# A second home for half of the attention outputs, and operand builds cut into casts and low parts

## The chip, the cores and the metric

The kernel runs on one core of a Trainium2 chip. The metric is device time in microseconds (us) of one execution. Before the change the median of three timed runs is 581.33 us (580.94 to 581.66).

The engines have short names in the profile: PE is TensorE (matrix products), PEld its weight loads, DVE is VectorE, ACT is ScalarE, POOL is GpSimd, and SP is SyncE, which here only issues transfers. Each engine runs its own instructions in the order in which the program lists them.

## The reference, cut to what matters

Attention with a decay goes over blocks and carries a state; its result x, with the heads side by side, goes through a mixer that works first over tokens and then over channels. All is float32.

```python
# attention: B=4, H=8, S=768, D=64; lam per head, about 0.97 to 0.99
for b in range(nb):                                   # blocks of 64 rows
    intra = (qb @ kb.T * Dmask) @ vb                  # Dmask[i, j] = lam ** (i - j), i >= j
    inter = (qb * lam_pow) @ kv_state
    out[:, :, sl] = intra + inter
    kv_state = lam_block * kv_state + (kb * rev_pow).T @ vb
# mixer: x is (4, 768, 512)
u  = x + (relu(x.T @ w_tok1) @ w_tok2).T              # 768 -> 256 -> 768, over tokens
h2 = relu(u @ w_ch1) @ w_ch2                          # 512 -> 1536 -> 512, over channels
return u + h2
```

## The kernel before, in words

Float32 values that go through the fast form of a matrix product (type fp32r) are split in two parts: a high part `...h`, which ScalarE makes as a cast, and a low part `...l`, the difference of the value and its high part, which VectorE or GpSimd makes. A product is then three products: high by high, high by low, low by high. Results lie transposed in the tiles `uT`, one for each of the 4 batches.

**Pairs.** The first stage goes over 16 pairs (batch, two heads), in the loop over `i` at L620. In step `i` TensorE computes the scores of pair `i + 1` (`sc`, L299), then the first half of the outputs of pair `i` (`xT`, three chunks of 128 rows, L323 and L333), then the state's products of the next pair (`kv`, L265), then the second half of the outputs (`outputs(i, 1)`). ScalarE copies each half from PSUM to `uT` (L340). VectorE scans the state's products (`sv`, L273). After that come transposes of later keys (`kt`, up to pair 7) and queries (`qt`, up to pair 4), transposes back of `uT` (`xp`, L355, read by ScalarE for `xhi` and VectorE for `xlo`), and pieces of the token mixer of earlier batches: `ph` (hidden, L447, read by ScalarE for `hh` and VectorE for `hl`) and `pu` (output, L484, added to `uT` by VectorE at L489). The list `groups` holds these pieces, and `take` says how many a step takes.

**PSUM.** There are eight banks. Three rotate under the tag `sh` (kt, qt, kv, xp, ph, pu, and later the products pa, pb, pc). One has the tag `xT`, used by both halves of the outputs and later by pd. Four are two double banks `sc`. A tile that takes a bank waits until the readers of the bank's last tile are done: under `sh` that is the tile three uses back, under `xT` the one before.

**Units.** The channel mixer is cut into 24 units (a group of 256 of the 1536 hidden channels, one batch): batches 0 and 1 in units 0 to 11, batches 2 and 3 in units 12 to 23. A unit multiplies two by two blocks with seven products (`m1` to `m7`) in place of eight. Their moving operands for a batch are B11, B21, B22, which are blocks of `uT`, and T1 to T4, which come from differences of blocks (`t1` to `t4`). The function `build` (L557) returns these steps, each as a call; `part` (L576) makes a high part on ScalarE and a low part on VectorE (`on_vector`) or GpSimd. For batches 2 and 3 the operands take the tiles of batches 0 and 1, and the differences lie in the tile `cs`, so their rows read `cs<-uT`. The products leave PSUM by s (a copy on ScalarE, L789), u2 and u3 (L794 and L807), c22, c21, c12 (VectorE, L812, L818, L823, all printed as `c`), and then become h11, h21, h12, h22 with their high and low parts. Between the products of unit n stand the four output pairs of unit n - 1 (`po`, L836, added to `uT` by VectorE at L851): m1, m6, pair 0, pair 1, m2, m7, m5, pair 2, m4, pair 3, m3. Pair 0 and pair 1 need h11 and h21, pairs 2 and 3 need h12 and h22. m2, m7 and m3 add to the banks of m1, m6 and m5, and wait until these have been read.

**What sets the order.** The order is written out by hand (a manual schedule). During the pairs a queue `waiting` holds small steps, and `later(n)` takes n from it, and one more when over five wait. In a unit `background(n)` gives a list of (when, step): a product counts 6 and an output pair 12, and a step is issued after the slot at which the count reaches its `when`. For batch 0 the steps are put in `waiting` at i = 13 (L701); for batch 1 they stand in the two lists named `order` (L712 and L734) and in units 0 and 1; for batches 2 and 3 in units 10 to 12 (NP1 is 12).

Of the kernel before, what the change touches and what calls it, by code (L numbers as in the profile page):

```python
# [22 lines left out]
def kernel(  # L23
# [40 lines left out]
    waiting = deque()  # L64

    def later(n):
        n += len(waiting) > 5
        for _ in range(min(n, len(waiting))):
            waiting.popleft()()

# [244 lines left out]
    def outputs(i, g):  # L315
        b, p = pairs[i]
        st = stb[i % 2]
        xT = bank("xT", f"xT{i}{g}", 3 * P)
        for cg in range(3):
            c = 3 * g + cg  # L320
            cs = slice(cg * P, (cg + 1) * P)
            for h in range(2):
                nc.tensor.matmul(  # L323
                    out=xT[h * D : (h + 1) * D, cs],
                    lhsT=vns[i][:, h, c, :],
                    rhs=weights_of[i, g, h][:, cg, :],
                    start=(cg == 0),
                    stop=False,
                )
            if c == 0:  # L330
                continue
            for h in range(2):
                nc.tensor.matmul(  # L333
                    out=xT[h * D : (h + 1) * D, cs],
                    lhsT=st[:, c - 1, h, :],
                    rhs=qss[i][:, c - 1, :],
                    start=False,
                    stop=(cg == 2),
                )
        nc.scalar.copy(out=uT[b][:, p, 3 * g * P : (3 * g + 3) * P], in_=xT)  # L340
# [216 lines left out]
    def build(b, n, temps=None, on_vector=()):  # L557
# [18 lines left out]
        def part(o, src):  # L576
            where = [home(n, o, x) for x in "hl"]
            ops[b][o] = hi, lo = [
                pool.tile([P, 2, SB], F32R, tag=tag, bufs=bufs, name=f"{o}{x}{b}")
                for x, (pool, tag, bufs) in zip("hl", where)  # L580
            ]
            nc.scalar.copy(out=hi, in_=src)
            eng = nc.vector if o in on_vector else nc.gpsimd
            eng.tensor_sub(out=lo, in0=src, in1=hi.bitcast(F32))

        return {
            "t1": lambda: temp("h", b12, b11),
            "t2": lambda: temp("l", b22, t["h"]),
            "t3": lambda: temp("m", b22, b12),
            "t4": lambda: sub(out=t["l"], in0=t["l"], in1=b21),  # L590
            "B11": lambda: part("B11", b11),
            "B21": lambda: part("B21", b21),
            "B22": lambda: part("B22", b22),
            "T1": lambda: part("T1", t["h"]),
            "T2": lambda: part("T2", t["l"]),
            "T3": lambda: part("T3", t["m"]),
            "T4": lambda: part("T4", t["l"]),
        }

    weights = {}  # L600
# [19 lines left out]
    for i in range(-2, NI):  # L620
# [28 lines left out]
        for n in range(3):  # L649
            for f in work[cuts[n] : cuts[n + 1]]:  # L650
                f()
                later(2 if len(work) < 3 else 1)
            if n < 2 and i >= 0:
                turn_back(i, n)
                later(1 if work or i == NI - 1 and n == 0 else 2 + n)
            if n == 0 and i + 2 < NI:
                scale_k(i + 2)
        if i == -1:
# [39 lines left out]
        if i == 11:  # L698
            later(99)
        if i == 13:  # L700
            waiting.extend(first[x] for x in ("t1", "t2", "T2", "T1", "t3", "T3", "t4", "T4", "B22"))  # L701
    later(99)
    att.close()
    ch = ctx.enter_context(tc.tile_pool(name="ch", bufs=1, reuse_waits="tile"))
# [4 lines left out]
        return cp.tile([P, SB], F32, tag="tmp", bufs=5, name=nm)  # L709

    parts = build(1, 1, on_vector=("T2", "T3"))
    order = [[parts["B11"]], [], [parts["t1"]], [parts["t2"], parts["B21"]]]  # L712
    for fs in order:
        groups.popleft()()
        for f in fs:
# [11 lines left out]
    def piece_steps(x):  # L727
# [4 lines left out]
    steps = {}  # L732
    pa = piece_steps(0)
    order = [  # L734
        [parts["T2"], pa[0]],
        [pa[1], pa[2], parts["T1"]],
        [pa[3], pa[4], parts["t3"], lambda: fetch(1, 2)],
        [parts["T3"]],
    ]
    for n, fs in enumerate(order):  # L740
        token_out_pair(B - 1, n // 2, 2 * (n % 2))
# [179 lines left out]
    def background(n):  # L921
# [7 lines left out]
        if n == 0:  # L929
            c1, pb = steps["c1"], piece_steps(1)  # L930
            add(12, pb[0], pb[1], c1[0])
            add(24, pb[2])
            add(36, parts["t4"])
            add(42, pb[3], pb[4], lambda: fetch(1, 3), c1[1])
        if n == 1:
            c1 = steps["c1"]
            add(12, parts["T4"])
            add(24, c1[2], c1[3], c1[4], c1[5])
            add(36, c1[6], parts["B22"])
# [32 lines left out]
                    add(84, lambda: save(to - 1))  # L972
        if n == NP1 - 2:
            second["a"] = bl = build(2, 0, cs_temps(), on_vector=("T1", "T2", "T3", "T4"))
            add(12, bl["t1"], bl["B11"])
            add(24, bl["t2"])
            add(36, bl["T2"])
            add(48, bl["t3"])
            add(60, bl["T3"])
            add(72, bl["T1"])  # L980
            add(84, bl["B21"])
        if n == NP1 - 1:
            al = second["a"]
            second["b"] = bl = build(3, 1, cs_temps(), on_vector=("T1", "T2", "T3", "T4"))
            add(6, al["t4"])
            add(12, al["T4"], al["B22"])
            add(24, bl["t1"], bl["B11"])
            add(36, bl["t2"])
            add(48, bl["T2"])
            add(72, bl["t3"], bl["T3"])  # L990
        if n == NP1:
            bl = second["b"]
            add(12, bl["T1"])
            add(24, bl["t4"])
            add(36, bl["T4"])
            add(36, bl["B21"])
            add(48, bl["B22"])
        if NP1 + 1 <= n < NP1 + 9:
            x = n - NP1 - 1
            add(36, lambda: store(x // 4, x % 4))  # L1000
# [75 lines left out]
```

## Time and profile before

| | |
|---|---|
| median of the runs | 581.33 us |
| the profiled execution's own time | 581.56 us |
| its span (first to last instruction) | 579.8 us |
| TensorE busy | 558.5 us, 96% |
| VectorE busy | 403.5 us, 70% |
| ScalarE busy | 215.9 us, 37% |
| GpSimd busy | 222.4 us, 38% |
| data moved to and from HBM | 67.1 MB, 116 GB/s over the span |

How to read its lines. A row of the waits says who waited for whom, how long in total, how often, and the longest. A row of a timeline has start and length in us, engine, line, operation, result<-inputs, shapes and count; in brackets is the engine's idle time ahead of it and what ended it. A row of the windows has the stretch, its length, and for PE, PEld, DVE, ACT and POOL the busy time with the count, then the share of TensorE's clock that was granted, the share in which the DMA engines were busy, and GB/s. The 16 pairs lie before 188 us of the span together with the token mixer, unit 0 starts at 187.91, unit 10 at 338.26, unit 13 at 389.31.

### The profile page before, as it was taken

To read this page: it belongs to the slowest core of one execution; us is meant where nothing else is said; L and a number is where in the kernel's file an instruction comes from. 1 tells how busy PE (TensorE), PEld (TensorE's weight loads), DVE (VectorE), ACT (ScalarE), POOL (GpSimd) and SP (SyncE) were. 2 spreads that over 40 slices of the span, in tenths; PEclk is the share of its full clock that TensorE was granted. 3 is DMA by queue.
4 is the path that set the end of the run, shared out by engine and by line. 5 is a ranking of instruction groups with operands and counts; after the bars stand their busy time and mean duration, and the time that the engine had idled before them with its cause. 6 is when DMAs were issued, how large, how long until landed. Compare 5 with 4: busy or idle time off the path is not lost. (4 is left out here: it accounts for less than half of the span.)

```text
span 579.8 us, 10666 instructions
## 1 busy us (share of the span) xinstructions
PE 558.5 (96%) x4234; PEld 540.3 (93%) x4234; DVE 403.5 (70%) x602; ACT 215.9 (37%) x426; POOL 222.4 (38%) x200
## 2 busy tenths in 40 slices
PE   5998999999989999999999998999999999999995
PEld 4888898999979999999999998999999999999994
DVE  4787877787777879887778787875455454444554
ACT  3464423435253554444434434451222222222221
POOL 5666632736214554534444453542112122222210
PEclk9998999999999999999999999999999999999999
DMA  9999999797002512352717200002444343540237
GB/s 184 258 227 187 190 198 215 138 161 141 1 2 83 216 71 86 128 217 58 288 38 272 73 0 1 0 1 47 136 115 134 97 147 93 153 101 1 42 48 129
DMA packets 176592, 67.80 MB, mean 117 GB/s; under 512 B 163616, under 2 KB 166816, under 8 KB 176544
## 3 DMA queue, kind: packets, MB, share of 16 engines
q1 hardware_dynamic: 172800, 65.85, 46.3%
q10 hardware_dynamic: 3744, 1.28, 0.9%
q8 instruction: 33, 0.54, 0.4%
q14 instruction: 15, 0.12, 0.1%
HBM read 49.29 MB, written 17.83 MB: 116 GB/s over the span
## 5 line engine op out<-in xcount | busy, mean ns | idle before, releaser
L851 DVE TENSOR_TENSOR uT<-po,uT 128x768 f32<-128x768 f32 x94 | 89.7, 955 | 70.1 <-PE po L836 69.8
L772 ACT ACTIVATE c<-c 128x384 f32<-128x384 f32 x72 | 37.9, 526 | 123.2 <-DVE c L812 54.4
L774 POOL TENSOR_TENSOR h22l<-c,h22h 128x384 fp32r<-128x384 f32 x24 | 25.0, 1040 | 127.8 <-ACT h22h L773 127.8
L286 POOL COPY stb<-sv 64x320 f32<-64x320 f32 x32 | 27.3, 853 | 45.0 <-DVE sv L273 44.1
L774 POOL TENSOR_TENSOR h21l<-c,h21h 128x384 fp32r<-128x384 f32 x24 | 27.4, 1142 | 32.9 <-ACT h21h L773 25.8
L774 POOL TENSOR_TENSOR h12l<-c,h12h 128x384 fp32r<-128x384 f32 x24 | 24.9, 1038 | 38.1 <-PE pa L761 19.2
L323 PE MATMUL xT<-a,vn 128*64 128x128 f32 x384 | 36.8, 284 | 1.8 <-ACT uT L340 1.4
L340 ACT COPY uT<-xT 128x384 f32<-128x384 f32 x32 | 15.3, 478 | 53.9 <-PE xT L333 53.9
L794 DVE TENSOR_TENSOR u<-pb,s 128x384 f32<-128x384 f32 x24 | 13.4, 557 | 28.9 <-PE pb L761 17.2
L307 DVE TENSOR_TENSOR a<-sc,mask 128x768 f32<-128x768 f32 x32 | 29.2, 950 | 6.1 <-PE sc L299 6.0
L800 ACT ACTIVATE h11h<-pa 128x384 fp32r<-128x384 f32 x24 | 11.7, 487 | 58.4 <-PE pa L761 58.4
L333 PE MATMUL xT<-qs,stb 128*64 128x128 f32 x320 | 31.8, 276 | 0.0
L447 PE MATMUL ph<-xhi,w1h 128*128 128x256 f32 x96 | 28.5, 297 | 1.8 <-DVE uT L489 1.5
L323 PEld LDWEIGHTS xT<-a,vn 128*64 128x64 f32 x384 | 22.4, 137 | 6.0 <-ACT uT L340 3.1
L375 POOL TENSOR_TENSOR c1l<-cs,c1h 128x512 fp32r<-128x512 f32 x15 | 19.3, 1296 | 21.8 <-ACT c1h L374 21.8
L299 PE MATMUL sc<-qT,kT 64*128 64x128 f32 x384 | 27.1, 290 | 0.2 <-ACT qT L237 0.2
L447 PE MATMUL ph<-xhi,w1l 128*128 128x256 f32 x96 | 27.1, 283 | 0.0
L447 PE MATMUL ph<-xlo,w1h 128*128 128x256 f32 x96 | 27.1, 282 | 0.0
L299 PEld LDWEIGHTS sc<-qT,kT 64*128 64x128 f32 x384 | 23.9, 196 | 3.3 <-issue 1.8
L252 POOL TENSOR_TENSOR qs<-qT,lamp 128x640 f32<-128x640 f32 x16 | 25.3, 1583 | 0.3
L364 DVE TENSOR_TENSOR xlo<-xp,xhi 128x384 fp32r<-128x384 f32 x32 | 17.6, 551 | 10.3 <-ACT xhi L363 10.3
L836 PE MATMUL po<-h21h,c2h 128*128 128x384 f32 x64 | 21.6, 338 | 0.7 <-ACT h21h L773 0.7
(273 smaller groups left out, 1884.1 us busy)
## 6 DMA issues: line engine op xcount, KB each, us to landing
raw<-in_moe_w_ch_dram SPq DMA_DIRECT2D x20, 512.0 KB, 4.0
vn<-in_v_dram SPq DMA_DIRECT2D x16, 384.0 KB, 5.2
kn<-in_k_dram SPq DMA_DIRECT2D x30, 192.0 KB, 4.7
out_dram<-y SPq DMA_DIRECT2D x110, 48.0 KB, 1.8
qn<-in_q_dram SPq DMA_DIRECT2D x44, 96.0 KB, 3.3
kr<-in_k_dram SPq DMA_DIRECT2D x32, 96.0 KB, 2.9
dc1h<-c1h SPq DMA_DIRECT2D x4, 768.0 KB, 6.0
dc1l<-c1l SPq DMA_DIRECT2D x4, 768.0 KB, 7.3
```

The lines of the kernel that those rows point to most:

```text
L252: nc.gpsimd.tensor_mul(out=qss[i], in0=qTs[i][:, P:].rearrange("p (c i) -> p c i", i=P), in1=lamp[:, p, None, :].broadcast_to([P, NC - 1, P]),
L286: nc.gpsimd.tensor_copy(out=st[r, :, h, :], in_=sv[r].rearrange("p (e c) -> p c e", c=NC - 1))
L299: nc.tensor.matmul(out=sc[h][:, c * P : (c + 1) * P], lhsT=kTs[i][r, cs], rhs=qTs[i][r, cs], start=True, stop=True,)
L307: nc.vector.tensor_mul(out=a, in0=pair.rearrange("p h (c i) -> p h c i", i=P), in1=mask[:, 2 * p : 2 * p + 2, None, :].broadcast_to([P, 2, ...
L323: nc.tensor.matmul(out=xT[h * D : (h + 1) * D, cs], lhsT=vns[i][:, h, c, :], rhs=weights_of[i, g, h][:, cg, :], start=(cg == 0), stop=False,)
L333: nc.tensor.matmul(out=xT[h * D : (h + 1) * D, cs], lhsT=st[:, c - 1, h, :], rhs=qss[i][:, c - 1, :], start=False, stop=(cg == 2),)
L375: nc.gpsimd.tensor_sub(out=lo, in0=src, in1=hi.bitcast(F32))
L447: nc.tensor.matmul(out=ph, lhsT=w[:, c, fs], rhs=x[:, c], start=(i == 0), stop=(i == 3 * NC - 1))
L772: nc.scalar.activation(src, src, AF.Relu)
L774: nc.gpsimd.tensor_sub(out=hl, in0=src, in1=hh.bitcast(F32))
L836: nc.tensor.matmul(out=to, lhsT=w[:, jj, t * P : (t + 1) * P], rhs=h, start=(i == 0), stop=(i == 3 * JG - 1))
L851: nc.vector.tensor_add(out=ub, in0=po, in1=ub)
```

## The change

The second half of each pair's outputs takes a bank under `sh` in place of the one under `xT`. `part` is cut in two: `part` issues the cast, a new function `low` the low part, and `build` returns three steps for each operand, `"T1"` (both), `"T1.h"` and `"T1.l"`. The lists that place the steps are written anew: for batch 0 in the queue, six bundles over pairs 14 and 15, with B22 moved behind the pairs; for batch 1 in the second `order` list and in units 0 and 1; for batches 2 and 3 in units 10 to 13. The extra step that `later` takes when over five wait stays only while more than 16 groups are left. No instruction is added or removed.

```diff
 def later(n):
-    n += len(waiting) > 5
+    n += len(waiting) > (5 if len(groups) > 16 else 99)
...
 def outputs(i, g):
-    xT = bank("xT", f"xT{i}{g}", 3 * P)
+    xT = bank("sh" if g else "xT", f"xT{i}{g}", 3 * P)
...
     def part(o, src):
...
         nc.scalar.copy(out=hi, in_=src)
+    def low(o, src):
+        hi, lo = ops[b][o]
         eng = nc.vector if o in on_vector else nc.gpsimd
         eng.tensor_sub(out=lo, in0=src, in1=hi.bitcast(F32))
-    return {
+    def both(o, src):
+        part(o, src)
+        low(o, src)
+    steps = {"B11": lambda: b11, ..., "T1": lambda: t["h"], "T2": lambda: t["l"], ...}
+    made = {o + s: lambda o=o, f=f: f(o, steps[o]()) for o in steps for s, f in (("", both), (".h", part), (".l", low))}
+    return made | {
...
-                later(1 if work or i == NI - 1 and n == 0 else 2 + n)
+                later(1 if work else 2 + n)
...
         if i == 13:
-            waiting.extend(first[x] for x in ("t1", "t2", "T2", "T1", "t3", "T3", "t4", "T4", "B22"))
+            for xs in (("t1",), ("t2", "T1.h"), ("T2.h", "T1.l"), ("T2.l", "t3", "t4"), ("T3.h", "T4.h"), ("T3.l", "T4.l")):
+                waiting.append(lambda xs=xs: [first[x]() for x in xs])
...
-    order = [[parts["B11"]], [], [parts["t1"]], [parts["t2"], parts["B21"]]]
+    order = [[first["B22"]], [parts["B11"]], [parts["t1"]], [parts["t2"], parts["B21"]]]
...
-        [parts["T2"], pa[0]],
-        [pa[1], pa[2], parts["T1"]],
-        [pa[3], pa[4], parts["t3"], lambda: fetch(1, 2)],
-        [parts["T3"]],
+        [parts["T2.h"], parts["T1.h"], pa[0]],
+        [parts["T2.l"], parts["T1.l"], pa[1], pa[2]],
+        [pa[3], pa[4], lambda: fetch(1, 2)],
+        [],
...
         if n == 0:
-            add(24, pb[2])
-            add(36, parts["t4"])
+            add(12, parts["t3"])
+            add(24, parts["T3.h"])
+            add(36, pb[2])
+            add(42, parts["T3.l"])
         if n == 1:
+            add(6, parts["t4"])
...
         if n == NP1 - 2:
-            add(12, bl["t1"], bl["B11"])
-            add(24, bl["t2"])
-            add(36, bl["T2"])
-            add(48, bl["t3"])
-            add(60, bl["T3"])
-            add(72, bl["T1"])
-            add(84, bl["B21"])
+            add(24, bl["t1"])
+            add(54, bl["t2"])
+            add(66, bl["B11"])
+            add(72, bl["T2.h"])
+            add(84, bl["T2.l"])
         if n == NP1 - 1:
-            add(6, al["t4"])
-            add(12, al["T4"], al["B22"])
-            add(24, bl["t1"], bl["B11"])
-            add(36, bl["t2"])
-            add(48, bl["T2"])
-            add(72, bl["t3"], bl["T3"])
+            add(6, al["t3"])
+            add(12, al["T3.h"])
+            add(24, al["T3.l"], al["T1.h"])
+            add(36, al["T1.l"])
+            add(42, al["t4"])
+            add(48, al["B21"])
+            add(54, al["T4.h"])
+            add(66, al["T4.l"])
+            add(72, al["B22"])
+            add(84, bl["t1"])
...
```

In units 12 and 13 batch 3's steps are spread in the same way: B11, t2, T2.h, T2.l, T1.h, T1.l, t3, T3.h with B21, T3.l and t4 in unit 12, and T4.h, T4.l and B22 in unit 13.

How this moves instructions, at three places. First TensorE in pair 5, from the state's products on, with what each instruction waits for (DVE_49 is a count of VectorE's instructions, and so on). Before:

```order
L265 MATMUL kv_891<-vn_687,kd_832 64x64 x8
L323 MATMUL xT_904<-a_713,vn_578 64x128 [waits Activation_49]
L323 MATMUL xT_904<-a_713,vn_578 64x128
L333 MATMUL xT_904<-qs_715,stb_119 64x128 x2
...
L216 MATMUL kt_921<-ident,kn_689 128x128 [waits DMAHW1_49,DMAHW0_49,DVE_49]
...
L216 MATMUL kt_926<-ident,kn_689 128x128 [waits DVE_49]
...
L355 MATMUL xp_935<-ident,uT_61 128x128 [waits DVE_49]
```

With the change:

```order
L265 MATMUL kv_891<-vn_687,kd_832 64x64 x8
L323 MATMUL xT_904<-a_713,vn_578 64x128 [waits DVE_49]
L323 MATMUL xT_904<-a_713,vn_578 64x128
L333 MATMUL xT_904<-qs_715,stb_119 64x128 x2
...
L216 MATMUL kt_921<-ident,kn_689 128x128 [waits DMAHW1_49,DMAHW0_49,DVE_49]
...
L216 MATMUL kt_926<-ident,kn_689 128x128 [waits DVE_49]
...
L355 MATMUL xp_935<-ident,uT_61 128x128 [waits Activation_49]
```

The order is the same. The second half of the outputs waits for VectorE's reading of a tile three uses back (an xp of pair 4) and no longer for ScalarE's copy. Each tile behind it now has another tile three uses back: the second kt has kv (read by the scan), where it had an xp, and xp has the outputs themselves (read by ScalarE).

Second VectorE in pairs 14 and 15, from the first difference of batch 0 (`th` is t1 and later t3, `tl` is t2 and later t4). Before:

```order
L574 TENSOR_TENSOR th_2198<-uT_60 128x768
L574 TENSOR_TENSOR tl_2200<-uT_60,th_2198 128x768
L364 TENSOR_TENSOR xlo_2203<-xp_2204,xhi_2202 128x3x128
L584 TENSOR_TENSOR T2l_2211<-tl_2200,T2h_2210 128x768
L584 TENSOR_TENSOR T1l_2215<-th_2198,T1h_2214 128x768
L489 TENSOR_TENSOR uT_62<-pu_2218,uT_62 128x384
L574 TENSOR_TENSOR th_2198<-uT_60 128x768
L452 SCALAR_TENSOR_TENSOR hl_2228<-ph_2229,hh_2227 128x256
L584 TENSOR_TENSOR T3l_2251<-th_2198,T3h_2250 128x768
L364 TENSOR_TENSOR xlo_2203<-xp_2254,xhi_2202 128x3x128
L590 TENSOR_TENSOR tl_2200<-tl_2200,uT_60 128x768
```

With the change:

```order
L574 TENSOR_TENSOR th_2198<-uT_60 128x768
L364 TENSOR_TENSOR xlo_2201<-xp_2202,xhi_2200 128x3x128
L574 TENSOR_TENSOR tl_2208<-uT_60,th_2198 128x768
L489 TENSOR_TENSOR uT_62<-pu_2213,uT_62 128x384
L587 TENSOR_TENSOR T1l_2211<-th_2198,T1h_2210 128x768
L452 SCALAR_TENSOR_TENSOR hl_2226<-ph_2227,hh_2225 128x256
L587 TENSOR_TENSOR T2l_2222<-tl_2208,T2h_2221 128x768
L574 TENSOR_TENSOR th_2198<-uT_60 128x768
L607 TENSOR_TENSOR tl_2208<-tl_2208,uT_60 128x768
L364 TENSOR_TENSOR xlo_2201<-xp_2251,xhi_2200 128x3x128
L452 SCALAR_TENSOR_TENSOR hl_2226<-ph_2263,hh_2225 128x256
L587 TENSOR_TENSOR T3l_2258<-th_2198,T3h_2257 128x768
```

The add of pu (L489) now stands ahead of both low parts, and T3's low part behind the second hl. T4's low part follows it, ahead of the next add of pu.

Third VectorE from the second half of unit 10 on (`u_10` is u3; the three `c_10` are c22, c21 and c12 in this order). Before:

```order
L584 TENSOR_TENSOR T2l_4120<-cs,T2h_4119 128x768
L801 SCALAR_TENSOR_TENSOR h11l_4130<-pa_4060,h11h_4129 128x384
L807 TENSOR_TENSOR u_10_4139<-pb_4069,s_10_4067 128x384
L574 TENSOR_TENSOR cs<-uT_62 128x768
L812 TENSOR_TENSOR c_10_4149<-pc_4142,u_10_4139 128x384
L851 TENSOR_TENSOR uT_61<-po_4156,uT_61 128x2x384
L584 TENSOR_TENSOR T3l_4171<-cs,T3h_4170 128x768
L818 TENSOR_TENSOR c_10_4181<-u_10_4139,pd_4174 128x384
L584 TENSOR_TENSOR T1l_4189<-cs,T1h_4188 128x768
L851 TENSOR_TENSOR uT_61<-po_4192,uT_61 128x2x384
L823 TENSOR_TENSOR c_10_4216<-pc_4142,u_10_4076 128x384
L590 TENSOR_TENSOR cs<-cs,uT_62 128x768
```

With the change:

```order
L812 SCALAR_TENSOR_TENSOR h11l_4121<-pa_4060,h11h_4120 128x384
L818 TENSOR_TENSOR u_10_4130<-pb_4069,s_10_4067 128x384
L823 TENSOR_TENSOR c_10_4139<-pc_4132,u_10_4130 128x384
L574 TENSOR_TENSOR cs<-uT_62,cs 128x768
L862 TENSOR_TENSOR uT_61<-po_4147,uT_61 128x2x384
L829 TENSOR_TENSOR c_10_4172<-u_10_4130,pd_4165 128x384
L862 TENSOR_TENSOR uT_61<-po_4182,uT_61 128x2x384
L587 TENSOR_TENSOR T2l_4180<-cs,T2h_4179 128x768
L834 TENSOR_TENSOR c_10_4203<-pc_4132,u_10_4076 128x384
L574 TENSOR_TENSOR cs<-uT_62 128x768
L805 TENSOR_TENSOR u_11_4227<-pb_4220,s_11_4217 128x384
```

T3's and T1's low parts, which stood ahead of c21 and of the next add, are gone to unit 11. t3 and T2's low part stand behind both, and of the operand steps only t2 is left between u3 and c21. On ScalarE in unit 0 the cast of T3 stood ahead of the copy s; now it stands behind h11's.

More of the change, by code (lines that the diff above doesn't have):

```diff
@@ L582, in part @@
             nc.scalar.copy(out=hi, in_=src)
+        def low(o, src):
+            hi, lo = ops[b][o]
             eng = nc.vector if o in on_vector else nc.gpsimd
             eng.tensor_sub(out=lo, in0=src, in1=hi.bitcast(F32))
-        return {
+        def both(o, src):
+            part(o, src)
+            low(o, src)
+        steps = {
+            "B11": lambda: b11,
+            "B21": lambda: b21,
+            "B22": lambda: b22,
+            "T1": lambda: t["h"],
+            "T2": lambda: t["l"],
+            "T3": lambda: t["m"],
+            "T4": lambda: t["l"],
+        }
+        made = {o + s: lambda o=o, f=f: f(o, steps[o]()) for o in steps for s, f in (("", both), (".h", part), (".l", low))}
+        return made | {
             "t1": lambda: temp("h", b12, b11),
@@ L590, in build @@
             "t4": lambda: sub(out=t["l"], in0=t["l"], in1=b21),
[L591 to L597, printed above, removed]
         }
@@ L984, in background @@
             second["b"] = bl = build(3, 1, cs_temps(), on_vector=("T1", "T2", "T3", "T4"))
-            add(6, al["t4"])
-            add(12, al["T4"], al["B22"])
-            add(24, bl["t1"], bl["B11"])
-            add(36, bl["t2"])
-            add(48, bl["T2"])
-            add(72, bl["t3"], bl["T3"])
+            add(6, al["t3"])
[8 more added lines that the diff above has]
+            add(84, bl["t1"])
         if n == NP1:
             bl = second["b"]
[L993 to L997, printed above, removed]
+            add(6, bl["B11"])
+            add(12, bl["t2"])
+            add(24, bl["T2.h"])
+            add(36, bl["T2.l"])
+            add(42, bl["T1.h"])
+            add(48, bl["T1.l"])
+            add(54, bl["t3"])
+            add(66, bl["T3.h"], bl["B21"])
+            add(72, bl["T3.l"])
+            add(84, bl["t4"])
+        if n == NP1 + 1:
+            bl = second["b"]
+            add(6, bl["T4.h"])
+            add(12, bl["T4.l"])
+            add(36, bl["B22"])
         if NP1 + 1 <= n < NP1 + 9:
```

## The prediction, made before the changed kernel ran

> **What bounds the kernel now.** I read the page first, then TensorE's waits, then windows cut at the channel units' first matmuls, then the timelines around each wait. The page says whose time counts:
>
> ```profile
> span 579.8 us, 10666 instructions
> PE 558.5 (96%) x4234; PEld 540.3 (93%) x4234; DVE 403.5 (70%) x602; ACT 215.9 (37%) x426; POOL 222.4 (38%) x200
> ```
>
> TensorE (PE) is busy for 96% of the span. Its instructions stand in the same order before and after, so the change can only move the time in which it stands still. Who it waits for (total us, times, longest):
>
> ```profile
> PE kv L265 <- DMA vn<-in_v_dram: 2.0, 1, 2.0
> PE ph L447 <- DVE uT L489: 1.5, 2, 1.0
> PE xT L323 <- ACT uT L340: 1.4, 2, 1.0
> PE po L836 <- ACT h21h L773: 0.7, 1, 0.7
> PE pa L761 <- ACT s L789: 0.7, 1, 0.7
> PE po L836 <- POOL h21l L774: 0.5, 1, 0.5
> PE po L836 <- DVE uT L851: 0.5, 2, 0.3
> PE pc L761 <- DVE c L812: 0.3, 1, 0.3
> ```
>
> Every edit has its rows here: xT waiting for uT (the bank), ph for uT (pairs 14 and 15), pa for s (unit 0), the po and pc rows (units 10 to 12). A wait costs more than its row, because matmuls overlap and a stop drains them. So I price the units by their length, from first matmul to first matmul, for units 9 to 12 (length, then busy time by engine):
>
> ```profile
> 322.43:338.26 15.83, 15.83 (x92) 15.83 (x91) 12.83 (x21) 6.65 (x13) 6.63 (x7) 1.00 0.10 34
> 338.26:354.49 16.23, 16.12 (x91) 15.81 (x91) 14.13 (x19) 6.46 (x13) 7.19 (x6) 1.00 0.00 0
> 354.49:373.00 18.51, 16.80 (x92) 15.52 (x91) 15.40 (x18) 9.03 (x15) 9.56 (x7) 1.00 0.00 1
> 373.00:389.31 16.31, 15.99 (x92) 15.67 (x91) 12.94 (x17) 8.79 (x15) 7.99 (x6) 1.00 0.00 1
> ```
>
> Unit 9 runs without a gap in 15.83. Units 10 to 12 take 51.05 in place of 3 x 15.83 = 47.49: 3.56 us lie there, for waits of about 2.1 in the table. Each of the six stops (h21h, h21l, two uT, two c) thus costs some 0.24 beyond its wait.
>
> **The change, part by part.**
>
> *A, the bank.* Both output halves of a pair used one xT bank, so the second waits until ScalarE (ACT) has copied out the first. With only the state's matmuls (kv) between them, that copy is always late. Pairs 4, 5 and 14:
>
> ```profile
> 47.82 0.80 PE L265 MATMUL kv<-vn,kd 128*64 128x64 f32 x20 [1.99 <-DMA vn<-in_v_dram]
> 48.42 0.42 PE L323 MATMUL xT<-a,vn 128*64 128x128 f32 x4
> ...
> 59.93 0.75 PE L265 MATMUL kv<-vn,kd 128*64 128x64 f32 x20
> 61.65 0.44 PE L323 MATMUL xT<-a,vn 128*64 128x128 f32 x4 [0.96 <-ACT uT L340]
> ...
> 62.12 0.81 DVE L273 TENSOR_TENSOR_SCAN sv<-keep,kv 128x320 f32<-128x320 f32 x1
> 63.10 0.64 PEld L216 LDWEIGHTS kt<-ident,kn 128*128 128x128 f32 x6 [0.17 <-DVE sv L273]
> ...
> 157.81 0.75 PE L265 MATMUL kv<-vn,kd 128*64 128x64 f32 x20
> 158.56 0.44 PE L323 MATMUL xT<-a,vn 128*64 128x128 f32 x4
> ```
>
> In pair 4 the bank had long been free (kv itself was late) and xT starts 0.60 after kv. In pair 14 it takes 0.75 with no gap drawn: TensorE has drained. In pair 5 it takes 1.72. In the rotating bank the second half waits for a tile three uses back, whose readers are done (in pair 15, xp of pair 14). Pairs 6 to 14 have 0.75 to 0.80, so each holds 0.15 to 0.20: 9 x 0.17 = 1.5. I set 0.2 off, since in a pair where VectorE (DVE) works without a pause from the state's scan on, the next bank comes free no earlier. Pair 5 would gain 1.72 - 0.60 = 1.1. But the rotation is now one tile fuller: its second kt needs kv's bank, which the scan frees at 62.12 + 0.81 = 62.93. Half of the six transposes (0.64) behind 63.10, it stood at about 63.45; so it gains 0.5 to 0.6, I take 0.5. Pairs 0 to 3 gain nothing, because kv at 47.82 waits for its transfer however early TensorE arrives. A = 1.5 - 0.2 + 0.5 = 1.8. Bounds: -0.3, if the fuller rotation stops two more groups at the price of kt's row (0.17), and 1.1 + 9 x 0.20 = 2.9.
>
> *B, pairs 14 and 15.* VectorE holds the bank that ph needs:
>
> ```profile
> 160.60 0.48 ACT L363 CAST xhi<-xp 128x384 fp32r<-128x384 f32 x1
> ...
> 161.72 0.55 DVE L364 TENSOR_TENSOR xlo<-xp,xhi 128x384 fp32r<-128x384 f32 x1
> ...
> 163.58 0.95 DVE L584 TENSOR_TENSOR T1l<-th,T1h 128x768 fp32r<-128x768 f32 x1
> 164.45 0.55 DVE L489 TENSOR_TENSOR uT<-pu,uT 128x384 f32<-128x384 f32 x1
> ...
> 163.60 0.49 PE L355 MATMUL xp<-ident,uT 128*128 128x128 f32 x3
> 165.05 0.39 PE L447 MATMUL ph<-xhi,w1h 128*128 128x256 f32 x1 [0.96 <-DVE uT L489]
> ...
> 170.40 0.44 PE L323 MATMUL xT<-a,vn 128*64 128x128 f32 x4 [0.46 <-ACT uT L340]
> ```
>
> The add of pu ends at 165.00. Now it stands ahead of both low parts, behind xlo and t2: xhi ends at 161.08, plus 0.55, 0.95 and 0.55 gives about 163.1. ph can start when xp's three transposes are through, near 163.95, so its 0.96 goes. The 0.46 before the second output of pair 15 goes by part A. With the restarts about 1.6. But T3's and T4's low parts now stand together ahead of the next add of pu, whose bank pair 15's second xp now needs. Behind the first add VectorE has T1l (to 164.0), hl, T2l (165.5), t3, t4 (167.3), xlo (167.8), then hl again, whose hh stands on ScalarE behind T4's cast (167.3 + 0.83), so near 169.0, then T3l, T4l and the add: 169.0 + 0.95 + 0.95 + 0.5 = 171.4. TensorE, 1.1 early from ph on and 0.5 more from xT, would want that bank near 171.0 in place of its 172.5 of before, so 0.4 comes back as a new wait. B = 1.2, between 0.3 (both low parts late by another 0.9) and 1.75 (no new wait).
>
> *C, unit 0.* The partial sum s is copied late, behind a cast that waits for t3 on VectorE:
>
> ```profile
> 188.57 0.95 DVE L574 TENSOR_TENSOR th<-uT 128x768 f32<-128x768 f32 x1
> 189.56 0.83 ACT L582 CAST T3h<-th 128x768 fp32r<-128x768 f32 x1 [5.84 <-DVE th L574]
> 190.30 0.47 ACT L789 COPY s<-pa 128x384 f32<-128x384 f32 x1
> ```
>
> Now t3 stands behind u2, and T3's cast behind h11's; s follows its matmuls, done near 189.1, and 0.67 plus a restart of 0.24 go. VectorE then runs late: t3 (0.95) stands between u2 and c22, which the last product must see read. Laid out, c22 is read 0.2 ahead of need. C = 0.9, between 0.3 (c22 and h21's low part 0.3 late each) and 0.95.
>
> *D, units 10 to 13.* Chains of cast and low part stood in one slot, and VectorE, a strict queue here, sat in them with the unit's own sums behind it:
>
> ```profile
> 355.16 1.14 DVE L584 TENSOR_TENSOR T3l<-cs,T3h 128x768 fp32r<-128x768 f32 x1 [1.01 <-ACT T3h L582]
> 356.23 0.54 DVE L818 TENSOR_TENSOR c<-u,pd 128x384 f32<-128x384 f32 x1
> ...
> 358.06 1.01 POOL L774 TENSOR_TENSOR h21l<-c,h21h 128x384 fp32r<-128x384 f32 x1 [2.57 <-issue]
> ```
>
> pd was complete near 352, yet c21 runs at 356.23, and h21h and h21l stop TensorE behind it. After the change c21 of unit 10 follows t2 and one add, near 351.2; h21l is done near 354 and wanted at about 357. In units 11 and 12 the same layout leaves c22 some four us, the adds about one, h21l over two. The work is the same less T4l, which moves on to unit 13. Nothing is late next, so the whole 3.56 goes, I take 3.5. Lower bound 1.9, if of the six stops the two longest (0.72 + 0.52, restarts 0.48) stay.
>
> Sum: 1.8 + 1.2 + 0.9 + 3.5 = 7.4. The profiled execution took 581.56 (the span and 1.8 around it), 0.2 above the median of 581.33. That gives 574.2 on its own scale, **573.9** for the median, with a span near 572.4.
>
> A rule against D: the Trainium skill, "SBUF — State Buffer", "Who interferes with whom", says that a VectorE instruction with two SBUF inputs and a GpSimd one that reads SBUF exclude each other for the whole instruction. The trace has such a pair:
>
> ```profile
> 343.31 2.11 POOL L584 TENSOR_TENSOR B11l<-uT,B11h 128x768 fp32r<-128x768 f32 x1 [0.59 <-ACT B11h L582]
> ...
> 343.64 2.60 DVE L574 TENSOR_TENSOR cs<-uT 128x768 f32<-128x768 f32 x1
> ```
>
> By that rule the row agrees, 2.60 beside GpSimd (POOL). Its result here is the last rival.
>
> **The rivals.** *R1, the rotation takes back what the bank gives* (0.12): scans, adds and copies on VectorE free the three banks just in time, so A falls to 0. For it speaks the quoted row in which kt's weights wait 0.17 for sv, against it that only pairs 0 to 5 have a kt, and the other tiles are read later. 573.9 + 1.8 = 575.7.
>
> *R2, the clock* (0.06). Behind the wait for vn the granted clock, the column after POOL's, is:
>
> ```profile
> 48.90:52.30 3.40, 3.40 (x28) 3.07 (x24) 2.55 (x4) 0.96 (x2) 2.23 (x3) 0.50 0.94 188
> ```
>
> TensorE stands 2.0 for vn, and then runs 3.4 us at half clock, which costs up to 1.7. Pairs 0 to 3 reach that wait up to 4 x 0.2 = 0.8 earlier, so it grows. If that brings a second such stretch: 575.6. The Trainium skill, "TensorE: Matmul & The Clock Gate", "What's actually happening", has the clock fall after a free-running idle window of about 3.4 us. The trace differs, since 2.0 us was enough.
>
> *R3, the stops of D move* (0.08) to another operand or add and half stays, for the low parts still stand in VectorE's queue between the unit's sums: 573.9 + 1.8 = 575.7.
>
> *R4, slower* (0.03): GpSimd's low parts fall beside VectorE's operand steps and VectorE bounds units 10 to 12. The busy time there of the six differences (L574) and of the eight low parts on VectorE (L584):
>
> ```profile
> sum 51.05, DVE 9.74; mean DVE 3.25
> sum 51.05, DVE 8.15 POOL 12.34; mean DVE 2.72 POOL 4.11
> ```
>
> That is 17.9 for 14 operations, 1.28 each, of VectorE's 14.13 + 15.40 + 12.94 = 42.5. At 2.60 each it would be 42.5 + 18.5 = 61.0, or 9.9 over today's 51.05; with A, B and C gained, 581.3 + 9.9 - 3.9 = 587.3. The unit gain is lost from 1.28 + (51.05 - 42.5) / 14 = 1.89 each, and the kernel is slower from 1.89 + 3.9 / 14 = 2.17. Against it, even the differences average 1.62 today, the low parts 1.02.
>
> **How the numbers follow.** Forecast 0.70, R1 0.12, R3 0.08, R2 0.06, R4 0.03, and 0.01 that nothing moves. The likeliest case reaches from 572.2 (all upper bounds: 2.9 + 1.75 + 0.95 + 3.56 = 9.2) to 575.2 (half of A and C gone, 1.35). R1 to R3 lie at 575.6 to 575.7, and two of them at once near 577.4. So 572.0 to 577.4 leaves out under 2 in 10. Under 0.2% (1.2 us) a measurement of this kernel cannot be told from no change; faster 0.95, same 0.02, slower 0.03.
>
> **What would show it.** Right: no wait of xT on uT and no PE waits on h21 or c; kv to xT 0.60 in pairs 6 to 14; s right behind pa; units 10 to 12 at 15.8 to 16.0 each; a short wait of xp on the add of pu in pair 15, and of kt on sv in pair 5. Wrong in A: xT still 0.75 behind kv with its bank free, or new rows of xp, pu or ph on sv. Wrong in B: ph on uT still near 1. Wrong in D: a unit over 16.5, or VectorE's 128x768 operations near 2 us each. The half-clock stretch longer than 3.4 us would be R2.

## The result, and the profile after

The changed kernel takes 572.81 us (median; 571.31 to 573.14) beside 580.94 (580.69 to 581.66) for the kernel before on the same chip: a ratio of 0.9854, 95% interval 0.9843 to 0.9865, or 8.1 us less. Forecast were 573.9 us, 7.4 less than 581.33. Lines behind L586 have moved down by 11 in the changed kernel (L761 is L772, L836 is L847, L818 is L829).

The page of the changed kernel, its line of the span and that of the engines:

```profile
span 570.7 us, 10676 instructions
PE 553.3 (97%) x4234; PEld 539.2 (94%) x4234; DVE 401.2 (70%) x602; ACT 216.0 (38%) x426; POOL 223.3 (39%) x200
```

TensorE runs the same 4234 instructions, and no engine has less work worth naming. TensorE's busy time still falls by 5.2, because a matmul drawn out by a stop counts as busy: in pair 14, kv to xT took 0.75 with no gap drawn, and takes 0.58 now. For whom it waits, from the waits of the changed kernel (total us, times, longest; the two rows of 0.2 left out):

```profile
PE kt L216 <- DMA kn<-in_k_dram: 5.4, 2, 5.1
PE kv L265 <- DMA vn<-in_v_dram: 2.2, 1, 2.2
PE kt L216 <- DVE sv L273: 0.9, 3, 0.5
PE yp L893 <- DVE uT L1065: 0.7, 1, 0.7
PE qt L236 <- DMA qn<-in_q_dram: 0.6, 1, 0.6
PE ph L447 <- DVE uT L489: 0.5, 1, 0.5
PE ph L447 <- DVE hl L452: 0.3, 1, 0.3
```

Of the rows that the prediction showed, those of xT for uT, pa for s, po for h21h, h21l and uT, and pc for c are gone, and of the two stops of ph the long one is. Two of the rows shown are new: kt waits for the scan sv, and at 12.76, in the start-up, qt waits 0.6 for a transfer. Units 9 to 12 in windows (length, busy time of PE, PEld, DVE, ACT and POOL, granted clock, DMA share, GB/s):

```profile
316.99:332.82 15.83, 15.83 (x92) 15.83 (x92) 12.83 (x21) 6.66 (x13) 6.59 (x7) 1.00 0.10 34
332.82:348.69 15.87, 15.87 (x91) 15.87 (x91) 12.18 (x19) 7.32 (x14) 8.89 (x7) 1.00 0.01 1
348.69:364.45 15.76, 15.76 (x91) 15.76 (x91) 12.23 (x17) 7.31 (x13) 4.82 (x4) 1.00 0.00 0
364.45:380.21 15.76, 15.76 (x91) 15.76 (x91) 13.25 (x16) 8.10 (x14) 10.33 (x7) 1.00 0.00 1
```

Units 10 to 12 take 47.39 where they took 51.05, and TensorE is busy from end to end. In the pairs the second output half now follows the state's matmuls in 0.58, in pair 5 and pair 14 alike (timeline of TensorE):

```profile
59.42 0.75 PE L265 MATMUL kv<-vn,kd 128*64 128x64 f32 x20
60.00 0.39 PE L323 MATMUL xT<-a,vn 128*64 128x128 f32 x4
...
61.41 0.55 PE L216 MATMUL kt<-ident,kn 128*128 128x128 f32 x3
62.47 0.33 PE L216 MATMUL kt<-ident,kn 128*128 128x128 f32 x1 [0.51 <-DVE sv L273]
...
155.37 0.75 PE L265 MATMUL kv<-vn,kd 128*64 128x64 f32 x20
155.95 0.39 PE L323 MATMUL xT<-a,vn 128*64 128x128 f32 x4
```

Taken from the starts of the same instructions in the two profiles, the time was won so: 0.51 ahead of the kv of pair 6 (start-up and transfers, which scatter from run to run), 0.43 in pair 5, 1.50 in pairs 6 to 13, 2.11 in pairs 14 and 15 up to unit 0, 0.93 in unit 0, 3.66 in units 10 to 12. That is 9.1 between the two profiled executions; the medians differ by 8.1, because the profiled execution of before lay 0.6 above its median and that of the changed kernel 0.3 below.

### The profile page after: what moved, and what is told of

Same layout as the page of the kernel before. It is cut to its first block, busy times and chain, and to the rows that moved or that the text cites. A ratio compares the mean times of both kernels' runs of the same rounds, so it can differ in the third digit from the quotient of the medians.

```text
span 570.7 us, 10676 instructions
## 1 busy us (share of the span) xinstructions
PE 553.3 (97%) x4234; PEld 539.2 (94%) x4234; DVE 401.2 (70%) x602; ACT 216.0 (38%) x426; POOL 223.3 (39%) x200
## 3 DMA queue, kind: packets, MB, share of 16 engines
q10 hardware_dynamic: 3744, 1.28, 0.9%
## 4 chain that ended last, share of the span: by engine, by line
PE 87%; DMA 5%; DVE 4%; ACT 1%; SPq 1%; issue 0%; ACTq 0%; DVEq 0%
PE po L847 35%; PE pa L772 9%; PE pc L772 9%; PE pb L772 9%; PE ph L447 6%; PE pd L772 4%; PE pu L484 3%; PE xT L323 3%; PE sc L299 3%; DMA qn<-in_q_dram 3%; PE xT L333 2%; DMA vn<-in_v_dram 2%; PE pu L467 1%; PE xp L355 1%; PE kv L265 1%; DVE a L307 1%
## 5 line engine op out<-in xcount | busy, mean ns | idle before, releaser
L847 PE MATMUL po<-h12h,c2h 128*128 128x384 f32 x64 | 21.6, 338 | 0.0
```

The costliest lines, as they stand in the source:

```text
L847: nc.tensor.matmul(out=to, lhsT=w[:, jj, t * P : (t + 1) * P], rhs=h, start=(i == 0), stop=(i == 3 * JG - 1))
```

## The experiments

| run | what it is | us | ratio to before [95%] |
|---|---|---|---|
| e1_bank | before, bank alone (A) | 578.49 | 0.9966 [0.9954, 0.9978] |
| e2_pairs | before, pairs 14 and 15 alone (B) | 578.47 | 0.9968 [0.9957, 0.9980] |
| e3_unit0 | before, units 0 and 1 alone (C) | 579.34 | 0.9986 [0.9977, 0.9996] |
| e4_units | before, units 10 to 13 alone (D) | 576.71 | 0.9936 [0.9922, 0.9950] |
| e5_strict | changed, banks strictly in turn | 572.04 | 0.9849 [0.9835, 0.9862] |
| e6_swap | changed, halves exchanged | 572.78 | 0.9866 [0.9848, 0.9883] |
| e9_joined | changed, low parts behind their casts | 571.51 | 0.9842 [0.9829, 0.9856] |
| e11_apart | before, low parts one slot later | 578.37 | 0.9958 [0.9946, 0.9971] |
| after_b | changed, once more | 571.97 | 0.9849 [0.9835, 0.9864] |
| e7_vn | changed, w_tok2 behind vn | 575.74 | 0.9914 [0.9900, 0.9927] |
| e10_third | changed, w_tok2 cut, 1.0 MB behind vn | 573.11 | 0.9868 [0.9847, 0.9889] |
| e12_after_kq | changed, 1.0 MB behind k and q too | 572.97 | 0.9869 [0.9851, 0.9887] |

### The four parts alone

e1 is one line; e2, e3 and e4 are the hunks of the change for their places, with the cut `part` and `low` that they need.

```diff
 e1_bank
-        xT = bank("xT", f"xT{i}{g}", 3 * P)
+        xT = bank("sh" if g else "xT", f"xT{i}{g}", 3 * P)
 e2_pairs: later(), the bundles at i == 13, B22 behind the first token output
 e3_unit0: the second `order` list, background(0) and background(1)
 e4_units: background(NP1 - 2) to background(NP1 + 1)
```

> The kernel before with the second output half in the three-bank pool and nothing else. Theory (the second half stood behind the copy of the first; part A): kv to xT falls from 0.75-0.85 to about 0.6 in pairs 6 to 14, pair 5 from 1.72 to about 1.2 with a wait of kt on the scan's sv in place of the rest, and the 0.46 before xT in pair 15 goes as well, while ph in pair 14 still waits about 1 for the add of pu. Unit 0 starts 2.3 to 2.7 us earlier, the whole is about 2.5 us shorter, ratio 0.9957. Rival (R1, the fuller rotation takes it back): other tiles of the pool stop for scans and adds in the same pairs, unit 0 starts under 0.8 us earlier, ratio 0.9985 to 1.000.

> The kernel before with the edits of pairs 14 and 15 alone (part B: the bundles of the first operand build, B22 behind the first token output, the threshold in later). Both output halves keep the single xT bank. Theory (ph waits for the add of pu, which stands behind low parts that wait for casts): ph's wait of 0.96 goes with its restart, pair 14 to unit 0 is 1.5 to 2.0 us shorter, ratio 0.9970; the wait of xT for uT in pair 15 stays at 0.1 to 0.4, since ScalarE has two casts ahead of that copy. If this part were worth only the 1.2 of the prediction (a new wait of 0.4 for xp on the add of pu), the ratio is 0.9979 and the wait is seen. Rival (the wait moves to another add of pu): under 0.5 us, ratio 0.9992.

> The kernel before with the edits of the last token outputs and units 0 and 1 alone (part C). Theory: s is copied right behind the matmuls of pa, the wait of 0.67 and its restart go, unit 0 shrinks from 8.27 to about 7.35 us, ratio 0.9984. Rival (VectorE is late, c22 or the low part of h21 stops the last products): unit 0 stays at 7.8 or more, ratio 0.9992 or above.

> The kernel before with the edits of units 10 to 13 alone (part D). Theory (casts and low parts in one slot held VectorE, and the unit's sums stood behind them): units 10 to 12 fall from 51.05 to about 47.5 us, 15.8 each, all waits for h21 and c go, ratio 0.9939. Rival R3 (half of the stops come back at other operands): units 10 to 12 at 49.3, ratio 0.9969. Rival R4 (GpSimd's and VectorE's operations beside each other): units 10 to 12 above 51, ratio above 1.

With 580.25 as the median of before in this set, the ratios are gains of 2.0 (A, 1.3 to 2.7), 1.9 (B, 1.2 to 2.5), 0.8 (C, 0.2 to 1.3) and 3.7 (D, 2.9 to 4.5). Their sum is 8.4; the whole change has 8.1 in its own set. The parts add up within the intervals, each wins by itself, and R1 and R3, in which A or half of D comes to nothing, are out.

The waits of TensorE from 150 us to unit 1, in e1 and then in e2, tell A and B apart:

```profile
PE ph L447 <- DVE uT L489: 1.2, 1, 1.2
PE pa L761 <- ACT s L789: 0.7, 1, 0.7
```

```profile
PE pa L772 <- ACT s L800: 0.7, 1, 0.7
```

With the bank alone, ph still waits for the add of pu, longer than before, since TensorE comes earlier. With the edits of the pairs alone that wait is gone, and so is the 0.46 of xT in pair 15, which I had expected to stay at 0.1 to 0.4. From kv of pair 6 to unit 0, A alone wins 2.43, B alone 1.87, and both 4.04. The missing 0.26 is, as I read it, part of that stop of 0.46, which either takes away. In e3 unit 0 shrinks to 7.34, and in e4 units 10 to 12 take 47.39, to the hundredth what they take in the changed kernel.

### Why the predicted wait in pair 15 did not come

The prediction had the second xp of pair 15 wait 0.4 for the add of pu, whose bank it took to be "three tiles back". In the changed kernel it did not wait for that add (weight loads of TensorE and VectorE's add):

```profile
167.91 0.55 DVE L489 TENSOR_TENSOR uT<-pu,uT 128x384 f32<-128x384 f32 x1
...
168.12 0.31 PEld L355 LDWEIGHTS xp<-ident,uT 128*128 128x128 f32 x3 [0.34 <-ACT uT L340]
```

The weight loads of the second xp start at 168.12 and its last matmul starts by 168.4, while the add ends at 168.46. So it cannot stand in pu's bank. The bank numbers in the built program say the same:

```
changed kernel, pair 15:  pu 1   xT(second half) 0   xp 2   xp 0   pu 1   pu 2
strictly in turn:         pu 2   xT(second half) 0   xp 1   xp 2   pu 0   pu 1
```

The pool rotates, but not always: banks are given out when the program is built, and here the second xp got the bank of the output half just copied, out of turn. Of the 206 tiles under `sh` in the changed kernel, only this xp and the pu behind it do not stand in the bank of the tile three uses back; of the 190 in the kernel before, none. That the pool goes by when it expects a bank to be free is my reading, which no run tests. e5 takes its choice away:

```diff
+        if tag == "sh":
+            turn[0] += 1
+            tag = f"sh{turn[0] % 3}"
-        return ps.tile([P, n], F32, tag=tag, bufs={"xT": 1, "sh": 3}[tag], name=nm)
+        return ps.tile([P, n], F32, tag=tag, bufs=1, name=nm)
```

> The changed kernel with the three banks of the pool handed out strictly in turn, in place of the pool's own choice. In the changed kernel the second xp of pair 15 got the bank of the output half just before it, not the bank of the add of pu three tiles back, on which the prediction had it wait 0.4 us. Theory (the bank was chosen otherwise, that is why the wait did not come): the second xp starts behind the add of pu, 0.3 to 0.6 later, unit 0 starts that much later, 0.4 us longer than the changed kernel. Rival (the wait did not come because VectorE reached the add early enough): the second xp starts within 0.1 of where it did, and nothing is longer. The ratio (0.9861 against 0.9854) cannot tell these apart, the rows of pair 15 can.

The same place in e5 (its lines stand 5 lower):

```profile
167.18 0.55 DVE L494 TENSOR_TENSOR uT<-pu,uT 128x384 f32<-128x384 f32 x1
...
167.87 0.52 PE L360 MATMUL xp<-ident,uT 128*128 128x128 f32 x3 [0.58 <-ACT xhi L368]
```

Now xp starts right behind the end of the add, 167.73, though the row names another releaser; 1.13 after the first xp (166.74) in place of 0.65. From kv of pair 15 to unit 0 it is 28.31 in place of 27.99. So the theory holds: the arithmetic of the wait was right, the premise about the bank was wrong. The 0.32 is too small for the ratio to show.

### Halves exchanged

```diff
-        xT = bank("sh" if g else "xT", f"xT{i}{g}", 3 * P)
+        xT = bank("xT" if g else "sh", f"xT{i}{g}", 3 * P)
```

> The changed kernel with the halves exchanged: the first output half in the three-bank pool, the second in the bank of its own. Both halves still have different banks, and the pool is as full. Theory (kt in pairs 2, 3 and 5 waits for the scan's sv because three tiles back of it is kv; now it is the first output half, copied earlier): kt's waits for sv (0.9 in all) go, pair 5 to 6 is 0.5 to 0.7 us shorter, ratio 0.9845. Rival (the pool's own fullness costs, whichever half is in it): another tile of pair 5 stops as long, ratio 0.9854. A mishap would show as waits of the first half for a tile that VectorE holds.

The waits of kt for sv do go, and nothing is won: kv of pair 6 to kv of pair 7 takes 11.38 in place of 11.36. Two rows of TensorE's timeline in pair 5 of e6 say where it went:

```profile
62.18 0.55 PE L355 MATMUL xp<-ident,uT 128*128 128x128 f32 x3 [0.19 <-DVE sv L273]
...
65.49 0.38 PE L447 MATMUL ph<-xhi,w1h 128*128 128x256 f32 x1 [0.29 <-DVE xlo L364]
```

xp and the second ph now stop for VectorE, which works from the scan on in the same order and no faster. From the scan's start on VectorE is busy for 5.76 of 5.80 us, in e6 as in the changed kernel. The rival holds: in pair 5 VectorE's queue is the bound, and kt's wait was only the first place where that showed.

### What in units 10 to 13 counts: apart, or in another order

The change did two things there: it set each low part apart from its cast, and it spread the steps over four units in a new order. e9 keeps the order and joins casts and low parts again; e11 keeps the old order and slots and only sets the low parts apart.

```diff
 e9_joined (for each of the eight)
-            add(72, bl["T2.h"])
-            add(84, bl["T2.l"])
+            add(72, bl["T2"])
 e11_apart (from before, for each of the eight)
-            add(36, bl["T2"])
-            add(48, bl["t3"])
+            add(36, bl["T2.h"])
+            add(48, bl["T2.l"], bl["t3"])
```

> The changed kernel in which each low part of T1 to T4 of units 10 to 13 stands right behind its cast again, in the cast's slot, with the new order and slots of the rest kept. Theory (it is the issuing apart that counts: VectorE stands through a cast of 0.83 us before each low part, with the unit's sums behind it): waits for h21, c or uT come back, units 10 to 12 take 0.5 to 2 us more than 47.4, ratio 0.9865 to 0.989. Rival (it is the new order and the spreading over four units that count, VectorE has time to stand through a cast): units 10 to 12 within 0.2 of 47.4, ratio 0.9854.

> The kernel before with units 10 to 13 in their old order and old slots, except that each low part of T1 to T4 stands one slot (two products) behind its cast. Nothing else of the change is in it. Theory (the stops come from VectorE standing through casts, so that either remedy, issuing apart or the new spread order, takes them away): units 10 to 12 fall from 51.05 to 47.4 to 48.2, ratio 0.9935 to 0.995. Rival (with the joined form in the new order at no loss, only the spread counts; the old slots crowd VectorE's queue ahead of the unit's sums whatever the casts do): units 10 to 12 stay at 49.5 to 51, ratio 0.997 to 1.000.

Units 10 to 12 of e9, then of e11, in windows:

```profile
sum 47.40, PE 47.40 PEld 47.40 DVE 38.41 ACT 22.62 POOL 22.80; mean PE 15.80 PEld 15.80 DVE 12.80 ACT 7.54 POOL 7.60
```

```profile
sum 48.89, PE 48.13 PEld 47.15 DVE 43.33 ACT 23.96 POOL 26.47; mean PE 16.04 PEld 15.72 DVE 14.44 ACT 7.99 POOL 8.82
```

With the new order, joining costs nothing: 47.40, beside 47.39. VectorE does stand for the casts in e9 (waits of VectorE in units 10 to 12):

```profile
DVE T2l L587 <- ACT T2h L582: 1.9, 1, 1.9
DVE T4l L587 <- ACT T4h L582: 1.9, 1, 1.9
```

but in these units TensorE has no wait long enough to be listed, so nothing that it needs soon is late behind them. In the changed kernel VectorE stands there too, 5.3 in all, for po. With the old order, setting apart alone wins 2.16 of the 3.66 (51.05 to 48.89) and leaves a stop of pc for c (0.44) and one of po for h21l (0.17). Neither statement of mine for e11 fits: it lies between. So the order was the sufficient part; setting apart is the weaker remedy, which the new order makes needless in these units.

### The stop for vn, which the change leaves

What is left in the pairs is kv's wait for vn and the stretch at half clock. The transfer of w_tok2 (1.5 MB) is ahead of that vn in SP's queue. Three kernels try other orders, beside the changed kernel once more.

```diff
 e7_vn
             load_v(i + 3)
+        if i == 2:
+            load_w2()
...
-        if i == 1:
-            load_w2()
 e10_third: load_w2(0) at i == 1 loads the first third, load_w2(1) behind load_v(5) the rest
 e12_after_kq: as e10, with load_w2(1) behind load_kq(6)
```

> The changed kernel with the transfer of w_tok2 issued behind pair 5's vn in place of ahead of it. Theory (kv's wait of 1.8 to 2.2 for vn, and where that wait is 2.0 or longer the 3.4 us at half clock behind it, come from 1.5 MB being ahead of vn in the queue): the wait is gone, TensorE has no stretch at half clock in any execution, 2 to 3.7 us shorter than the changed kernel, ratio 0.980 to 0.982. Rival (the wait only moves: VectorE then waits about 1 us for w_tok2 in its conversion and is late with the weights of the scores, or kt waits for its kn, which stands behind w_tok2): under 0.6 us gained, ratio 0.9845 or above.

> The changed kernel with the transfer of w_tok2 cut: the third that the first conversion reads (0.5 MB) is issued where the whole was, the other 1.0 MB behind pair 5's vn. Theory (vn waits behind 1.5 MB; VectorE's conversion needs only the first third by 46 us and the second not before 58): vn lands about 2.5 us earlier, kv's stop of 1.8 to 2.2 shrinks to under 0.5, no stretch at half clock, and no new stop of VectorE or ScalarE: 2 us shorter than the changed kernel, 2.7 where the yardstick's executions have the stretch; ratio 0.981 to 0.983. Rival (as with the whole transfer behind vn, another wait takes over: kn of the next pair or a VectorE that is itself the bound of pairs 4 and 5): gain under 0.6, ratio 0.9845 or above.

> The changed kernel once more, as the yardstick for the two kernels beside it on the same chip: ratio 0.9854 again, 0.984 to 0.987. TensorE's stop before kv of pair 5 differs between executions (1.8 to 2.2 us in the profiles so far), with or without a stretch at half clock behind it, which moves a single profile by up to 1.7 us.

> The changed kernel with w_tok2 cut as before (the third that the first conversion reads stays where the whole was), and the other 1.0 MB issued behind pair 6's k and q in place of ahead of them. With the cut alone kv had no stop, but kt of pair 6 stood 2.4 us for its kn, which was behind the 1.0 MB. Theory (the order in the queue decides who is late; the 1.0 MB is read by ScalarE not before about 52 and has time): neither vn nor kn is late, no stretch at half clock, the scan frees kt's bank in time, unit 0 starts 2 to 4 us earlier than in the changed kernel, ratio 0.979 to 0.982. Rival (the transfers as a whole are the bound up to there: what is moved back comes late itself): ScalarE's first step on the second third waits 1 us or more for w_tok2, with xhi and the copies behind it, or the next vn, kn and qn are late; gain under 0.6, ratio 0.9845 or above.

All three let kv run without a stop, at 44.9 to 45.4 in place of 47.26, and none is faster than the changed kernel; e7 is slower. The stop comes back at kt of pair 6, a little over 2 us later in the program. The half clock comes back with it: a stretch of 6.83 us in e7 and of 3.41 in e10 and e12, where I had expected none. TensorE's waits of e7, of e10 and of e12, one or two rows of each:

```profile
PE kt L216 <- DVE uT L386: 3.5, 1, 3.5
PE kt L216 <- DVE sv L273: 2.8, 4, 1.9
```

```profile
PE kt L216 <- DMA kn<-in_k_dram: 7.8, 3, 5.0
```

```profile
PE kt L216 <- DVE sv L273: 4.0, 4, 2.9
```

In e7 VectorE stands 3.46 for w_tok2 in its conversion, and the weights of the scores and the scan are queued behind it; I had taken the transfer to land about 1 us late. In e10 the next kn is late, behind the 1.0 MB (2.4 of the row's 7.8; the rest belongs to the start, as in the changed kernel). In e12 no engine waits for a transfer from 42 to 72 us, and kt waits for the scan all the same: the rival's number holds there (nothing is won), but not its reason, a late transfer. VectorE's timeline in e12, then in the changed kernel, says why:

```profile
46.24 1.67 DVE L386 SCALAR_TENSOR_TENSOR uT<-uT,uT 128x512 uint32<-128x512 uint32 x1
47.84 1.81 DVE L307 TENSOR_TENSOR a<-sc,mask 128x768 f32<-128x768 f32 x2
49.57 0.80 DVE L273 TENSOR_TENSOR_SCAN sv<-keep,kv 128x320 f32<-128x320 f32 x1
```

```profile
45.97 0.43 DVE L383 TENSOR_SCALAR uT<-uT 128x512 uint32<-128x512 uint32 x1 [0.20 <-DMA uT<-in_moe_w_tok_dram]
46.43 1.63 DVE L386 SCALAR_TENSOR_TENSOR uT<-uT,uT 128x512 uint32<-128x512 uint32 x1
47.99 1.81 DVE L307 TENSOR_TENSOR a<-sc,mask 128x768 f32<-128x768 f32 x2
49.72 0.80 DVE L273 TENSOR_TENSOR_SCAN sv<-keep,kv 128x320 f32<-128x320 f32 x1
```

The scan starts at 49.57 or 49.72 whether kv ran at 44.87 or at 47.26, because VectorE has work right up to it: a conversion, two products for the scores, the scan. The one pause among these rows is the 0.20 for w_tok2 in the changed kernel. From 40 to 52 us VectorE is busy for 11.86 of 12 in e12 and for 11.39 in the changed kernel, by the windows. kt needs the bank that the scan frees. So the 2.2 for vn and most of the half clock lie beside VectorE's queue and are worth little by themselves. One place to look is the conversion step at L386: beside GpSimd's w1l and qs it takes 1.63 and 1.67, and 0.69 in e7, where it runs behind them. No run moved VectorE's or GpSimd's steps there, so whether that helps stays open, and no version here can be told to beat the changed kernel: the intervals of e5 and e9 overlap its own.

## Why the prediction was right, and where its sum was not

- **What bounds the kernel.** Right: TensorE's order is the same, and the gain is time in which it no longer stands or is drawn out by a stop. Of the six stops in units 10 to 12 the table of waits shows five; the sixth, of pc for c at 353.34, has a gap of only 0.11.
- **A, 1.8 forecast, 2.0 measured alone, 2.1 in the profile** (0.43 in pair 5, 1.50 in pairs 6 to 13, 0.17 in pair 14). Alone, A also takes away the stop of 0.46 in pair 15, which the forecast has under B. The 0.17 for each pair came in pairs 6 to 14, though unevenly (nothing between the kv of pairs 11 and 12, 0.29 between those of pairs 14 and 15), and pair 5 gave 0.43 for a forecast 0.5, with the new stop of kt for sv (0.51) as said. The 0.2 that I set off for VectorE's late scans was not needed. Kv to xT is 0.58 where I said 0.60. What pairs 0 to 3 gave cannot be told from the scatter of the transfers ahead of pair 6.
- **B, 1.2 forecast, 1.9 measured alone.** This is the term that was mis-sized: the changed kernel's two pairs gain 2.11, of which 0.17 are A's, and the 1.94 left exceed the upper bound of 1.75. The step that failed reads "whose bank pair 15's second xp now needs": xp had another bank, and the 0.4 never came back (with the banks in turn, in e5, it is 0.32). The rest of the step holds by its times: the add of pu ends at 160.73, which with the lead of 2.44 at that place is 163.17 on the old clock, forecast 163.1. ph then started 0.24 behind xp, where I had 0.35.
- **C, 0.9 forecast, 0.8 alone, 0.93 in the profile.** s starts at 184.60, 1.24 behind the first matmul of pa, and unit 0 takes 7.34. c22 ends 0.15 ahead of the matmul that needs it, forecast 0.2.
- **D, 3.5 forecast, 3.7 alone, 3.66 in the profile.** All six stops went. c21 of unit 10 starts at 345.79, which with the lead of 5.44 is 351.2 on the old clock, as forecast. What I did not see is that the order alone does it: my reason, "Chains of cast and low part stood in one slot" with "the unit's own sums behind it", names both a cast and a queue, and e9 shows that the queue counts.
- **R2, the clock** (0.06). No second stretch in the pairs: 3.41 us at half clock after as before. My price of up to 1.7 for one stretch was too high: the changed kernel's execution without it (after_b) starts unit 0 only 0.6 earlier (182.73 for 183.36), since kt then waits 0.99 for the scan in place of nothing.
- **R4, slower** (0.03). The operations did not grow. In units 10 to 12 of the changed kernel, by the windows of their lines, six differences take 6.43 and the seven low parts that stay there on VectorE 8.30: 1.13 each where before it was 1.28, far from 1.89. The slow rows are not gone from the chip, they are gone from this order: in e11, with the old slots, t1 still takes 2.60 beside GpSimd's B22l.

The sum was 0.7 short of the measured 8.1, and none of its terms was too high by the profile. There the four come to 8.6: A is 0.3 above its forecast, B 0.7, D 0.2. Of B's 0.7 the wait that did not come makes 0.4 and ph's earlier start 0.1; the rest is spread over pairs 14 and 15. With the 0.51 ahead of pair 6 the two profiled executions are 9.1 apart, which is more than the 8.1 of the medians and no better measure of the change. The forecast time missed by 1.1, 573.9 for 572.81; the other 0.4 is the median of before, 580.94 in this set for 581.33.

## What to carry to other kernels

Before costing a wait for "the tile n uses back", look up which buffer the tile really got: a pool may hand them out out of turn. When a small step stalls the engine it runs on, ask what stands behind it in the queue; moving it to a place where nothing urgent follows did more here than splitting it, and made the splitting needless. And before removing the longest wait of the bottleneck, check the second engine there: if that works without a pause to the same instant, the wait only changes its name.

## What the runs showed of the hardware that was not expected

The half clock depends on more than the length of the stop. A stop of kv of 1.94 or shorter was followed by no stretch in all seven profiles that have one (1.7 to 1.94, e1 to e4, e9, e11 and after_b). Longer ones were followed by one in the kernel before (1.99), the changed kernel (2.22), and e6 (2.11), and so were the stops of kt in e7, e10 and e12 (2.4 to 3.5), but not the stop in e5, which was 2.22 as well. TensorE at half clock in the changed kernel (window, granted clock in the third column from the right):

```profile
47.32:50.73 3.41, 3.41 (x44) 0.50 1.00 178
```

Where the stop lies decides. The trace's record of the full clock begins at 9.76 us in the changed kernel (three transposes kt take 0.87 ahead of that, six take 0.88 behind it), at 11.34 in the kernel before, at 9.61 in e6 and at 8.92 in e5. The stretches of the first three begin 37.55 behind that, which is 11 times 3.413; those of e7, e10 and e12 begin 40.96 behind it, 12 times. So I cut the traces into windows of 3.413 from there. The window ahead of the stretch in the changed kernel, then the two windows that share e5's stop (length, busy time of TensorE, granted clock, DMA share, GB/s):

```profile
43.89:47.31 3.42, 1.20 (x22) 1.00 0.96 204
```

```profile
43.05:46.47 3.42, 2.10 (x36) 1.00 1.02 246
46.47:49.88 3.41, 2.51 (x47) 1.00 0.98 176
```

In the changed kernel TensorE stands for 2.22 in one window. In e5 the stop, from 45.15 to 47.37, is cut at 46.47 into 1.32 and 0.90, and the clock stays. Over all windows of the fourteen profiles, up to the end of each span, every one at full clock in which TensorE stands for 1.99 or more is followed by half clock, none with 1.79 or less is, and of the two in between, 1.92 in e3 is not and 1.91 near the end of e12 is. So e5 is no exception, and whether a stop of about 2 us brings the stretch depends on how the windows cut it.

The Trainium skill, "TensorE: Matmul & The Clock Gate", "What's actually happening", speaks of a window of 3.4 us that runs on its own, so that the same kernel meets it at different points. The length of 3.41 and the two outcomes at 2.22 agree with that; that stops of 2 us were enough does not agree with an idle window of 3.4.
